# x blocks in the four-block output products, and group 0 on the same scheme: a fused attention and maxout kernel

## The chip, the cores and the metric

The kernel runs on one core of a Trainium2 chip. Its engines work side by side, each through its own instructions in order: TensorE (PE, matrix products), VectorE (DVE), ScalarE (ACT), GpSimd (POOL), and SyncE (SP), which here only issues transfers. PE's weight loads are listed apart as PEld. The metric is the device time of one execution in microseconds.

## The reference

Attention first, token by token, over 4 batches, 8 heads, 768 tokens and a head dimension of 48; then a feed-forward part over the 3072 tokens, with d_model 384 and d_ff 768:

```python
f = 1.0 / (1.0 + np.exp(-f_logit))
for t in range(S):
    state = f[:, :, t, :, None] * state + np.einsum('bhd,bhe->bhde', k[:, :, t], v[:, :, t])
    y[:, :, t] = np.einsum('bhd,bhde->bhe', q[:, :, t], state)
x = y.transpose(0, 2, 1, 3).reshape(B * S, H * D)
h = np.maximum(np.maximum(x @ w1, x @ w2), x @ w3)
out = h @ w_out
```

## The kernel before

**Units and groups.** Attention is cut into 24 units u of 128 rows (64 tokens of two batches). Four units make a group g of 512 tokens, and the feed-forward part works group by group, one group behind the attention: while the units 8 to 11 are worked, PE also does the feed-forward part of group 1, and so on. Group 0's part (`ffn_first`) is spread over the startup and the units 4 to 7; group 5's runs alone at the end.

**A unit** goes through `scan` (DVE, L329), `after` and `before` (the decays into keys and queries; POOL L340, L351, DVE L347), `pairs` (PE L392, DVE L395 applies the mask: tile at), `values` (PE L411), `sums` (PE L436, the state's increment), `finish` (PE L500) and `pack`. `sums` multiplies by ks, the keys by tokens, which DVE makes by 32x32 transposes in `keys_by_blocks` (L382): a unit has four blocks n of four transposes, the blocks 2 and 3 of unit u being made while unit u is worked, and L436's first two matmuls need blocks 0 and 1, the third needs block 3.

**The feed-forward weights.** The three input weights lie in w_in[0..2], six blocks of 128 columns each. w_in[1] and w_in[2] are stored less w_in[0], so that max(x w1, x w2, x w3) = x w1 + max(0, x w2', x w3'). The part x w1 is linear and goes straight to the output: `linear` multiplies w1 by w_out (PE L745) into w_nat, and w_lin is w_nat with its rows in the order of the packed x. So the output of a group is hm @ w_out + x @ w_lin, where hm holds the maxima, in six blocks of 128. Weights can arrive as pairs of 32-bit words; they are rounded on the chip by `round_begin` and `round_end` in 24 pieces, 18 of w_in and 6 of w_out: for pieces from number 3 on with two ACT operations (L240, L241) and one of DVE (L254), for the pieces below with two of DVE (L251, L252); then POOL adds (L258).

**Seven products for eight.** In groups 1 to 5 a product is taken two blocks by two blocks with Strassen's scheme in Winograd's form: seven block products, with sums of blocks made ahead. `inputs_by_pairs` does so for hm (PE L836; steps named start, plain, fifth, sixth, seventh, third, fourth for each of the three block pairs n). `fourth(n)` ends a pair: DVE takes the two maxima (L886, L887), and POOL makes four sums of the pair's blocks (`sums_of_hm`, L596, 128x256 each, into the places s1, s2, s4 in w_in[1] and into the blocks themselves). `outputs_by_pairs` (PE L609) then multiplies hm by w_out in seven products, with three hm pairs each, and adds x @ w_lin by four plain products of three x blocks each. The banks a, b and c of PSUM take the products in an order in which one bank's sum is used on: ACT reads bank a out (`read`, L614), while the next product is added on the same bank; DVE (`add`, L617) and POOL (L662) add the parts into the output. The weights' differences (w_mix) are made once by `mix` (POOL, L587).

**Group 0** uses plain products (`product`, PE L537; the maxima DVE L767), then `linear`, then `outputs` (PE L563), nine matmuls of 128x384 for each of four units, with `mix_in` and `mix` on POOL beside them.

**What sets the order.** It is written out by hand. The feed-forward part is a generator that yields the cost of each step; `fill(ns)` draws steps from it until a budget is used up, and stands between the steps of the units. The budgets are EARLY for units 4 to 7 and PART after. Every engine's queue keeps the order in which the program issues, so DVE works its maxima, its transposes and its scans strictly one after the other.

Of the kernel before, what the change touches and what calls it, by code (L numbers as in the profile page):

```python
# [46 lines left out]
C = 64  # L47
# [8 lines left out]
def kernel(  # L56
# [33 lines left out]
    def fast():  # L90
        ctx = ExitStack()
        with ctx:
# [137 lines left out]
            BY_VECTOR = 3  # L230
# [3 lines left out]
            def round_begin(n):  # L234
                if n in raw:
                    lo, hi = words(n)
                    top = tops[:, n % 4].bitcast(U32)
                    if n >= BY_VECTOR:

                        nc.scalar.activation(top.bitcast(FP32), hi.bitcast(FP32), AF.Sign)  # L240
                        nc.scalar.mul(top.bitcast(FP32), top.bitcast(FP32), -2.0)  # L241

                    rest = rests[:, n % 3].bitcast(U32)
                    nc.scalar.activation(rest, lo, AF.Copy, scale=2.0 ** -29)
                    halfway[n] = (top, rest)

            def round_end(n):
                if n in raw:
                    (top, rest), (_, hi) = halfway.pop(n), words(n)
                    if n < BY_VECTOR:  # L250
                        nc.vector.tensor_scalar(top, hi, 3, 0x3FFFFFF8, op0=ALU.logical_shift_left, op1=ALU.bitwise_and)  # L251
                        nc.vector.scalar_tensor_tensor(top, hi, 0xC0000000, top, op0=ALU.bitwise_and, op1=ALU.bitwise_or)  # L252
                    else:
                        nc.vector.scalar_tensor_tensor(top, hi, 3, top, op0=ALU.logical_shift_left, op1=ALU.bitwise_xor)  # L254

                    dst = pieces[n][0].bitcast(U32)
                    by = lambda t: t.rearrange("p (a c) -> p a c", a=dst.shape[1])
                    nc.gpsimd.tensor_tensor(dst, by(top), by(rest), op=ALU.add)  # L258
                    raw.pop(n)
# [250 lines left out]
            def by_halves(xT):  # L510

                return xT[:, 0:NK].rearrange("p k t -> p (k t)").rearrange("p (two k t) -> p two k t", two=2, k=NK)
# [14 lines left out]
            def bank(in_tr=False):  # L527
                if in_tr:
                    return ps_tr.tile([128, TOK], FP32, name="tr")
                return ps_f.tile([128, TOK], FP32, name="p")  # L530
# [26 lines left out]
            def outputs(hm, xT, i):  # L557
                p = bank()
                t = slice(i % 2 * UT, (i % 2 + 1) * UT)
                terms = [(hm[:, j, i * UT:(i + 1) * UT], w_out[:, j, :]) for j in range(NJ)]  # L560
                terms += [(by_halves(xT)[:, i // 2, k, t], w_nat[:, k, :]) for k in range(NK)]
                for n, (lhsT, rhs) in enumerate(terms):
                    nc.tensor.matmul(p[:, 0:DM], lhsT=lhsT, rhs=rhs, start=(n == 0), stop=(n == NJ + NK - 1))  # L563
                    if n % NK == NK - 1:
                        if n == NJ + NK - 1:
                            o = o_four[:, i]
                            nc.scalar.copy(o, p[:, 0:DM])
                            store(i, o)
                        yield NK * DM * COLUMN

            HJ, HD = NJ // 2, DM // 2
            corner = lambda k, n: w_out[:, k::2, n * HD:(n + 1) * HD]
            w_mix = [keep.tile([128, HJ, HD], FP32, name="mix")] + [w_in[2][:, :, n * HD:(n + 1) * HD] for n in range(4)]
            s_mix = [w_in[1][:, n, :].rearrange("q (jj t) -> q jj t", jj=HJ) for n in range(NK)]
            partial = [w_in[0][:, n, 0:DM] for n in range(NK)]
            pairs_of = lambda t: t.rearrange("q (p c) -> q p c", p=2)  # L580

            def mix(n):

                dst, x, y = ((w_mix[2], corner(1, 1), corner(0, 1)), (w_mix[0], corner(0, 1), corner(0, 0)),
                             (w_mix[1], corner(1, 1), w_mix[0]), (w_mix[3], corner(1, 0), w_mix[1]),
                             (w_mix[4], w_lin[:, :, 0:HD], w_lin[:, :, HD:]))[n]
                nc.gpsimd.tensor_tensor(dst, x, y, op=ALU.subtract)  # L587

            def sums_of_hm(hm, jj):

                first, second = ([hm[:, 2 * jj + k].rearrange("q (p n t) -> q n p t", p=2, n=2)[:, n] for n in range(2)]
                                 for k in range(2))
                s1, s2, s4 = (pairs_of(t[:, jj]) for t in s_mix)
                for dst, x, y, op in ((s1, first[1], second[1], ALU.add), (s2, s1, first[0], ALU.subtract),
                                      (first[1], first[0], first[1], ALU.subtract), (s4, second[0], s2, ALU.subtract)):
                    nc.gpsimd.tensor_tensor(dst, x, y, op=op)  # L596

            def outputs_by_pairs(g, hm, xT):
                tile_of = lambda p, n: slice((2 * p + n) * UT, (2 * p + n + 1) * UT)
                A = lambda k, n: lambda p: hm[:, k::2, tile_of(p, n)]  # L600
                X = lambda n: lambda p: xT[:, 0:NK, tile_of(p, n)]
                s1, s2, s4 = (lambda p, t=t: t[:, :, p * UT:(p + 1) * UT] for t in s_mix)
                lin = [w_lin[:, :, n * HD:(n + 1) * HD] for n in range(2)]
# [3 lines left out]
                def into(b, p, lhs, rhs):  # L607
                    for k in range(HJ):
                        nc.tensor.matmul(b[:, p * HD:(p + 1) * HD], lhsT=lhs(p)[:, k], rhs=rhs[:, k],  # L609
                                         start=id(b) not in begun, stop=(k == HJ - 1), skip_group_check=True)  # L610
                        begun.add(id(b))

                def read(b, n):
                    nc.scalar.copy(partial[n], b[:, 0:DM])  # L614
# [4 lines left out]
                COST = HJ * HD * COLUMN  # L619
                a, b, c = bank(), bank(True), bank(True)  # L620
                into(b, 0, X(0), lin[0])
                yield COST
                into(b, 1, X(0), lin[0])
                yield COST
                into(a, 0, A(0, 0), corner(0, 0))
                yield COST
                into(b, 0, A(1, 0), corner(1, 0))
                yield COST
                into(a, 1, A(0, 0), corner(0, 0))
                read(a, 0)  # L630
                yield COST
                into(b, 1, A(1, 0), corner(1, 0))
# [3 lines left out]
                yield COST  # L636
                into(a, 0, s2, w_mix[1])
                yield COST
                into(a, 1, s2, w_mix[1])
                read(a, 1)  # L640
                yield COST
                d = b if last else c
                into(c, 0, s1, w_mix[0])
# [4 lines left out]
                into(d, 1, s1, w_mix[0])  # L648
# [5 lines left out]
                into(a, 0, A(0, 1), w_mix[2])  # L654
                yield COST
                into(a, 1, A(0, 1), w_mix[2])
                yield COST
                into(a, 0, X(1), lin[1])
                yield COST
# [3 lines left out]
                if last:  # L663
                    store_part(g, 1, 1)
                yield COST
                into(c, 0, X(0), lin[1])
                yield COST
                into(d, 1, X(0), lin[1])
                yield COST
                into(a, 0, A(1, 1), w_mix[3])  # L670
                yield COST
                into(a, 1, A(1, 1), w_mix[3])
# [3 lines left out]
                into(a, 0, X(1), w_mix[4])  # L676
                yield COST
                into(a, 1, X(1), w_mix[4])
# [3 lines left out]
                yield COST  # L682
                into(c, 0, s4, corner(1, 1))
# [3 lines left out]
                into(d, 1, s4, corner(1, 1))  # L687
# [67 lines left out]
            def ffn_first(xT):  # L755
# [18 lines left out]
                for a in range(NK):  # L774
                    if a < 2:
                        for n in range(2 * NK + 2):
                            place(placed[a].bitcast(FP32), w_in[a + 1], n)
                    for cost in linear(a):
                        round_to(rounded[0] + 1)
                        yield cost  # L780
                for n in range(2 * NK + 2):
                    place(w_lin, w_nat, n)
                made = iter([lambda n=n: mix_in(n) for n in range(4)] + [lambda n=n: mix(n) for n in range(5)])
                for i in range(GRP):
                    for n, cost in enumerate(outputs(hm, xT, i)):
                        if i or n:
                            next(made, lambda: None)()
                        if i == GRP - 1 and n == 1 and 1 in packed:
                            sums_of_x(1)
                        yield cost  # L790
# [33 lines left out]
            def inputs_by_pairs(g, hm, xT):  # L824
# [57 lines left out]
                def fourth(n):  # L882
                    into(A[n], n, w_two[1][:, 1], t4)
                    yield COST
                    into(A[n], n, w_two[1][:, 2], t5)
                    nc.vector.scalar_tensor_tensor(out(n, 0), out(n, 0), 0.0, two(A[n]), op0=ALU.max, op1=ALU.max)  # L886
                    nc.vector.scalar_tensor_tensor(out(n, 1), out(n, 1), 0.0, u3, op0=ALU.max, op1=ALU.max)  # L887
                    sums_of_hm(hm, n)
                    yield COST
# [48 lines left out]
            EARLY = 2360  # L938
            PART = (33 * TOK + 22 * HJ * HD) * COLUMN / (5 * GRP)
# [408 lines left out]
```

## Time and profile before

| | |
|---|---|
| median of 3 runs | 423.31 us (423.26 to 423.86) |
| the profiled execution's own time | 423.43 us |
| its span, first to last instruction | 421.7 us |
| PE busy | 402.8 us, 96% |
| DVE, POOL, ACT busy | 264.5, 235.2, 180.2 us |
| group 0's outputs | 98.2 to 127.06 us |
| group 1, 2, 3 | to 187.47, 247.98, 308.49 us |
| group 4, group 5 | to 366.10, 416.60 us |

The stages are read from the timeline by PE's lines: a group goes from its first input product (L836) to the last output product (L609). The granted clock of PE is 0.996 over the span. A matmul of the program with 32-bit operands shows as two records in the trace. A row of the timeline gives start, duration, engine, line, operation, written and read tiles, and behind "x" how many records it gathers; in brackets stand the idle time of the engine ahead of it and what ended that.

### The profile page before, as it was taken

How to read it: one execution, taken by the hardware profiler on the slowest of the kernel's cores; microseconds unless marked ns; L12 is line 12 of the kernel's file. 1: busy time of each engine (PE TensorE's matmuls, PEld its weight loads, DVE VectorE, ACT ScalarE, POOL GpSimd, SP SyncE). 2: the span in 40 equal slices, each digit the busy share in tenths (PEclk: the TensorE clock that was granted, in tenths of full speed). 3: DMA queues.
4: the chain of work that ended last, by engine and by line, in shares of the span. 5: the costliest groups of instructions: out<-in, count | busy, mean ns of one | idle time of the engine just before them, and what ended most of it. 6: DMA issues, size and time to landing. Idle time of an engine off the chain costs nothing.

```text
span 421.7 us, 11556 instructions
## 1 busy us (share of the span) xinstructions
PE 402.8 (96%) x4650; PEld 338.5 (80%) x4650; DVE 264.5 (63%) x515; ACT 180.2 (43%) x414; POOL 235.2 (56%) x262
## 2 busy tenths in 40 slices
PE   4978899899999999999999999999999999999995
PEld 3756765466668888998889988889988889988994
DVE  6986594843597699868789867889764730002300
ACT  2478676632114442425531444442254524576210
POOL 2189554621988676376586357576556960435600
PEclk9999999999999999999999999999999999999998
DMA  8999897782547654277645276635473010542002
GB/s 169 232 266 284 236 258 112 121 170 67 102 85 129 87 116 66 60 106 101 117 104 95 56 113 87 144 79 89 64 144 91 11 54 9 158 140 75 2 19 60
DMA packets 175129, 47.20 MB, mean 112 GB/s; under 512 B 154016, under 2 KB 172768, under 8 KB 175072
## 3 DMA queue, kind: packets, MB, share of 16 engines
q1 hardware_dynamic: 171600, 45.61, 52.0%
q10 hardware_dynamic: 3472, 0.81, 0.9%
q8 instruction: 37, 0.61, 0.6%
q14 instruction: 20, 0.16, 0.1%
HBM read 37.75 MB, written 4.72 MB: 101 GB/s over the span
## 4 chain that ended last, share of the span: by engine, by line
PE 86%; SPq 5%; DVE 3%; POOL 2%; issue 1%; ACT 1%; DMA 1%; DVEq 0%; POOLq 0%
PE p L836 19%; PE tr L836 16%; PE p L609 15%; PE tr L609 12%; PE p L563 6%; PE p L537 5%; PE p L745 3%; PE y L500 3%; PE y L411 3%; SPq L164 2%; PE a L392 2%; SPq L174 2%; PE y L436 2%; POOL w_in L258 1%; DMA placed<-in_moe_w_dram 1%
## 5 line engine op out<-in xcount | busy, mean ns | idle before, releaser
L836 PE MATMUL tr<-xT,placed 128*128 128x256 f32 x300 | 73.3, 385 | 0.0
L382 DVE STREAM_TRANSPOSE ks<-kh 32x128 f32<-32x128 f32 x224 | 67.7, 302 | 4.6 <-POOL kh L340 1.0
L836 PEld LDWEIGHTS tr<-xT,placed 128*128 128x128 f32 x300 | 55.6, 190 | 9.1 <-ACT hm L844 1.4
L836 PE MATMUL p<-xT,placed 128*128 128x256 f32 x180 | 45.0, 381 | 0.0
L537 PE MATMUL p<-xT,w_in 128*128 128x256 f32 (+1 forms) x108 | 34.4, 459 | 4.9 <-DVE hm L767 2.2
L836 PEld LDWEIGHTS p<-xT,placed 128*128 128x128 f32 x180 | 33.8, 190 | 4.7
L329 DVE TENSOR_TENSOR_SCAN r<-gate,from_one 128x520 f32<-128x520 f32 x24 | 31.3, 1306 | 8.9 <-ACT gate L308 5.9
L617 DVE TENSOR_TENSOR o<-tr,w_in 128x384 f32<-128x384 f32 (+1 forms) x11 | 5.7, 515 | 48.8 <-PE tr L609 43.5
L340 POOL TENSOR_TENSOR kh<-kt,r 128x512 f32<-128x512 f32 x16 | 28.7, 1796 | 10.6 <-DVE kt L296 10.6
L596 POOL TENSOR_TENSOR w_in<-hm 128x256 f32<-128x256 f32 x15 | 10.9, 727 | 40.5 <-DVE hm L887 40.5
L854 POOL TENSOR_TENSOR hm<-hm,rest_bits 128x512 f32<-128x512 f32 x15 | 22.7, 1514 | 19.2 <-ACT hm L844 19.2
L506 ACT COPY xT<-y 64x256 f32<-64x256 f32 (+1 forms) x60 | 22.1, 369 | 24.1 <-PE y L500 23.4
L347 DVE TENSOR_TENSOR_SCAN prod<-gate,from_inv 128x520 f32<-128x520 f32 x24 | 31.9, 1329 | 0.0
L395 DVE TENSOR_TENSOR at<-a,mask 128x512 f32<-128x512 f32 x24 | 16.5, 688 | 24.2 <-PE a L392 23.9
L836 PE MATMUL p<-w_in,placed 128*128 128x256 f32 x120 | 30.0, 379 | 0.0
L537 PEld LDWEIGHTS p<-xT,w_in 128*128 128x128 f32 x108 | 19.3, 190 | 13.0 <-issue 6.2
L258 POOL TENSOR_TENSOR w_in<-top_bits,rest_bits 128x384 uint32<-128x384 uint32 x18 | 21.8, 1218 | 13.5 <-DVE top_bits L254 8.0
L879 DVE TENSOR_TENSOR hm<-tr,hm 128x512 f32<-128x512 f32 x15 | 10.2, 681 | 29.3 <-PE tr L836 19.3
L662 POOL TENSOR_TENSOR o<-top_bits,w_in 128x384 f32<-128x384 f32 x5 | 5.1, 1018 | 41.6 <-ACT w_in L614 41.6
L614 ACT COPY w_in<-p 128x384 f32<-128x384 f32 x15 | 7.2, 480 | 47.3 <-PE p L609 47.3
L280 ACT ACTIVATE raw<-top_bits 128x384 f32<-128x384 f32 x48 | 25.3, 526 | 0.4
L836 PEld LDWEIGHTS p<-w_in,placed 128*128 128x128 f32 x120 | 22.8, 190 | 3.1
(155 smaller groups left out, 888.4 us busy)
## 6 DMA issues: line engine op xcount, KB each, us to landing
raw<-in_moe_w_dram SPq DMA_DIRECT2D x24, 384.0 KB, 4.2
v_ld<-in_v_dram SPq DMA_DIRECT2D x48, 96.0 KB, 3.3
placed<-in_moe_w_dram SPq DMA_DIRECT2D x12, 384.0 KB, 5.7
out_dram<-o SPq DMA_DIRECT2D x46, 96.0 KB, 2.2
placed<-in_moe_w_out_dram SPq DMA_DIRECT2D x6, 384.0 KB, 5.9
raw<-in_moe_w_out_dram SPq DMA_DIRECT2D x6, 384.0 KB, 3.3
f_ld<-in_f_logit_dram SPq DMA_DIRECT2D x32, 64.0 KB, 2.6
k_ld<-in_k_dram SPq DMA_DIRECT2D x32, 64.0 KB, 2.5
```

The costliest lines, as they stand in the source:

```text
L258: nc.gpsimd.tensor_tensor(dst, by(top), by(rest), op=ALU.add)
L280: nc.scalar.activation(over, size, AF.Relu, scale=(-1 / HI_MIN, 1.0)[step - 1], bias=(1.0, -HI_END * (1 - 2.0 ** -24))[step - 1], accum_ou ...
L329: nc.vector.tensor_tensor_scan(r[:, 0:LEN][:, ::-1], flat(gate)[:, ::-1], flat(from_one)[:, ::-1], 1.0, op0=ALU.mult, op1=ALU.max)
L340: (nc.vector if u < BY_ROWS else nc.gpsimd).tensor_tensor(kh.rearrange("p h a t -> p a h t"), kt, by_batch(r[:, 1:LEN + 1].rearrange("p (x ...
L347: nc.vector.tensor_tensor_scan(flat(prod), flat(gate_tiles[u % 2]), flat(from_inv[u % 2]), 1.0, op0=ALU.mult, op1=ALU.max)
L382: nc.vector.transpose(ks[n * 32:(n + 1) * 32, :, par, e0:e0 + 32], kh[p0:p0 + 32, :, a, t0:t0 + 32])
L506: nc.scalar.copy(xT[o, :, t0 + a * C:t0 + (a + 1) * C], y[i, a, 0:HP * C].rearrange("p (h t) -> p h t", h=HP))
L537: nc.tensor.matmul(p if w < TOK else p.rearrange("p (two t) -> p two t", two=2), lhsT=w_in[i][:, kt, j * 128:(j + 1) * 128], rhs=x[:, t.st ...
L563: nc.tensor.matmul(p[:, 0:DM], lhsT=lhsT, rhs=rhs, start=(n == 0), stop=(n == NJ + NK - 1))
L609: nc.tensor.matmul(b[:, p * HD:(p + 1) * HD], lhsT=lhs(p)[:, k], rhs=rhs[:, k], start=id(b) not in begun, stop=(k == HJ - 1), skip_group_c ...
L836: nc.tensor.matmul(b[:, j * HALF:(j + 1) * HALF], lhsT=w[:, (2 * n + j) * 128:(2 * n + j + 1) * 128], rhs=x, start=begin and j == 0, stop= ...
L854: nc.gpsimd.tensor_tensor(out(n, 0), out(n, 0), first, op=ALU.add)
```

## The change

In the groups 1 to 5 the first two of the three x blocks become a fourth block pair in each of the seven output products: their sums are made like those of hm (`sums_of_pair`), on DVE, two in `fourth(1)` and two in `fourth(2)`; the differences of w_lin's blocks are made in group 1 by `mix_x`, on DVE. The third x block stays plain. In the two first hm products the blocks of the last hm pair stand behind those of all others ("early" and "rest"). The s1 product now stands before the s2 product.

Group 0 drops `outputs` and uses `outputs_by_pairs` with x plain, with its hm sums made during `linear` and its stores put out later, by `store_late` in group 1. `mix` goes from POOL to DVE, right behind `linear`, and `mix_in` goes into four steps of group 0's outputs. The w_out pieces are rounded by the two-operation way of DVE, two pieces a step. EARLY goes from 2360 to 2270, and PART follows the new number of products.

```diff
-            BY_VECTOR = 3
+            BY_VECTOR = (*range(3), *range(3 * NJ, 4 * NJ))
...
-                nc.gpsimd.tensor_tensor(dst, x, y, op=ALU.subtract)
+                nc.vector.tensor_tensor(dst, x, y, op=ALU.subtract)
+
+            def mix_x(n):
+
+                of = lambda k, c: w_lin[:, k, c * HD:(c + 1) * HD]
+                dst, x, y = ((x_mix[2], of(1, 1), of(0, 1)), (x_mix[0], of(0, 1), of(0, 0)),
+                             (x_mix[1], of(1, 1), x_mix[0]), (x_mix[3], of(1, 0), x_mix[1]),
+                             (w_mix[4][:, 2], of(2, 0), of(2, 1)))[n]
+                nc.vector.tensor_tensor(dst, x, y, op=ALU.subtract)
+
+            def sums_of_pair(x0, x1, *sums, part=slice(0, 4), engine=nc.gpsimd):
+
+                first, second = ([x.rearrange("q (p n t) -> q n p t", p=2, n=2)[:, n] for n in range(2)] for x in (x0, x1))
+                s1, s2, s4 = (pairs_of(t) for t in sums)
+                for dst, x, y, op in ((s1, first[1], second[1], ALU.add), (s2, s1, first[0], ALU.subtract),
+                                      (first[1], first[0], first[1], ALU.subtract), (s4, second[0], s2, ALU.subtract))[part]:
+                    engine.tensor_tensor(dst, x, y, op=op)
...
+                mixed = g > 0
+                order = [*range(HJ - 1), *[HJ] * mixed, HJ - 1]
+                A = lambda k, n: lambda p: [(xT[:, k] if jj == HJ else hm[:, 2 * jj + k])[:, tile_of(p, n)] for jj in order]
...
-                into(a, 0, A(0, 0), corner(0, 0))
-                yield COST
-                into(b, 0, A(1, 0), corner(1, 0))
-                yield COST
-                into(a, 1, A(0, 0), corner(0, 0))
+                early, rest = slice(len(order) - 1), slice(len(order) - 1, None)
+                for p in range(2):
+                    into(a, p, A(0, 0), C(0, 0), early)
+                    yield COST - PART_COST
+                    into(b, p, A(1, 0), C(1, 0), early)
+                    yield COST - PART_COST
+                for p in range(2):
+                    into(a, p, A(0, 0), C(0, 0), rest)
                 read(a, 0)
...
-                into(a, 0, s2, w_mix[1])
-                yield COST
-                into(a, 1, s2, w_mix[1])
-                read(a, 1)
-                yield COST
                 d = b if last else c
-                into(c, 0, s1, w_mix[0])
+                into(c, 0, s1, T(0))
...
+                into(a, 0, s2, T(1))
                 yield COST
-                into(a, 1, A(0, 1), w_mix[2])
+                into(a, 1, s2, T(1))
+                read(a, 1)
+                yield COST
+                into(a, 0, A(0, 1), T(2))
...
-                    for cost in linear(a):
-                        round_to(rounded[0] + 1)
+                    for n, cost in enumerate(linear(a)):
+                        round_to(rounded[0] + 2)
+                        if a and n < 2:
+                            jj = 2 * (a - 1) + n
+                            if jj < HJ:
+                                sums_of_hm(hm, jj)
                         yield cost
...
-                for i in range(GRP):
-                    for n, cost in enumerate(outputs(hm, xT, i)):
...
+                for n in range(5):
+                    mix(n)
+                for n, cost in enumerate(outputs_by_pairs(0, hm, xT)):
+                    if 3 <= n < 7:
+                        mix_in(n - 3)
+                    yield cost
...
                     sums_of_hm(hm, n)
+                    if n:
+                        sums_of_pair(xT[:, 0], xT[:, 1], *s_of_x(xT), part=slice(2 * n - 2, 2 * n), engine=nc.vector)
+                    if g == 1:
+                        for i in range(3 * n, min(3 * n + 3, 5)):
+                            mix_x(i)
                     yield COST
...
-            EARLY = 2360
-            PART = (33 * TOK + 22 * HJ * HD) * COLUMN / (5 * GRP)
+            EARLY = 2270
+            PART = (33 * TOK + 64 * HD) * COLUMN / (5 * GRP)
```

## The prediction

> **What bounds the kernel now.** First the page's busy shares, then the chain that ended last, then PE's waits, then the stretches of the program, and last the timeline around the place where the change puts its new work. The page says that PE is the bound, and that VectorE (DVE) is not, on average:
>
> ```profile
> PE 402.8 (96%) x4650; PEld 338.5 (80%) x4650; DVE 264.5 (63%) x515; ACT 180.2 (43%) x414; POOL 235.2 (56%) x262
> ...
> PE 86%; SPq 5%; DVE 3%; POOL 2%; issue 1%; ACT 1%; DMA 1%; DVEq 0%; POOLq 0%
> ```
>
> The answer on stretches, one line for the group 3 (group 2 reads the same), shows no idle time of PE at all, and DVE at 49.24 of 60.51 us:
>
> ```profile
> 247.98:308.49 60.51, 60.51 (x777) 53.99 (x777) 49.24 (x107) 23.93 (x56) 37.76 (x41) 1.00 0.55 96
> ```
>
> So a matmul less is time less, and a wait that PE does not have now is time more. The timeline where group 3's outputs begin (start, duration, engine, line) shows how close the nearest wait is:
>
> ```profile
> 280.10 0.69 DVE L879 TENSOR_TENSOR hm<-tr,hm 128x512 f32<-128x512 f32 x1 [0.70 <-PE tr L836]
> ...
> 280.80 1.26 DVE L382 STREAM_TRANSPOSE ks<-kh 32x128 f32<-32x128 f32 x4
> ...
> 282.81 2.11 PE L609 MATMUL tr<-w_in,xT 128*128 128x192 f32 x12
> ...
> 284.83 0.68 DVE L886 SCALAR_TENSOR_TENSOR hm<-hm,p 128x512 f32<-128x512 f32 x1
> 285.43 0.68 DVE L887 SCALAR_TENSOR_TENSOR hm<-hm,top_bits 128x512 f32<-128x512 f32 x1
> 285.56 0.30 PEld L609 LDWEIGHTS p<-w_out,hm 128*128 128x128 f32 x2 [0.28 <-DVE hm L886]
> ...
> 286.14 1.28 DVE L382 STREAM_TRANSPOSE ks<-kh 32x128 f32<-32x128 f32 x4
> 286.25 0.72 POOL L596 TENSOR_TENSOR w_in<-hm 128x256 f32<-128x256 f32 x1 [3.93 <-DVE hm L887]
> 287.06 0.74 POOL L596 TENSOR_TENSOR w_in<-w_in,hm 128x256 f32<-128x256 f32 x1
> ...
> 287.58 0.63 PE L436 MATMUL y<-v_ld,ks 64*64 64x48 f32 x32
> ...
> 288.09 1.48 DVE L347 TENSOR_TENSOR_SCAN prod<-gate,from_inv 128x520 f32<-128x520 f32 x1
> ...
> 288.43 1.67 POOL L596 TENSOR_TENSOR w_in<-hm,w_in 128x256 f32<-128x256 f32 x1
> ```
>
> Three things are to be seen. From 280.10 to 287.42 DVE has no gap: third maximum (L879), transposes, at, gate, scan, reciprocal, L886, L887, transposes. The last four transposes end at 287.42, and PE's L436, which multiplies by their result, starts at 287.58: a margin of 0.16 us. And the last POOL sum takes 1.67 instead of 0.73, ending 0.53 after DVE's scan: two engines, both reading two SBUF operands, took turns.
>
> **The change, part by part.** Durations are of the profiled execution, whose time is 423.43 us (span 421.7), 0.1 above the median 423.31. I forecast on 423.43 and count the 0.1 as nothing; 0.2%, or 0.85 us, is about what a measurement here can tell from no change.
>
> 1. *Fewer matmuls, groups 1 to 5.* A program matmul of 128x192 is two records; twelve records take 1.95 us in the chain ("171.29 1.95 PE tr L609 x12"), so 0.325 each. 64 instead of 66 in each of five groups: 10 x 0.325 = **-3.25**.
> 2. *Group 0.* 36 matmuls of 128x384 at 6.00 us for 18 records, nine matmuls ("101.77 6.00 PE p L563 x18"): 0.667 each, 24.0. Now 66 x 0.325 = 21.45: **-2.55**. Its hm sums (12 POOL sums of 0.73) go into the linear part from 87 us on; the five mixes, now on DVE at 0.5 to 0.7 (an estimate from L254's 0.55 for 128x384 and L617's 0.55), lie at 95.9 to 100.3, where DVE stands idle 6.88 before its L395 at 101.84. The eight late stores of group 0 on SP stand behind v loads that are wanted a unit later. All of this is hidden by PE's outputs; uncovered it would be some 3 us.
> 3. *A later read of the last hm pair.* L886's 0.28 wait in the timeline, in groups 1 to 3 (six matmul records take 1.39 instead of 1.14): 3 x 0.25 = **-0.75**. The last pair's matmuls now come behind L411 and L436.
> 4. *Startup.* EARLY moves the fills; PE's stall of 0.92 at 74.64 behind DVE's L767 should go. Against that, rounding of the six w_out pieces takes two DVE operations (L251 0.60, L252 0.56) for one (L254, 0.55 to 0.80). Between -1.2 and 0, and I take **-0.6**.
> 5. *Reads of bank a that lose their cover.* A read by ACT between two products on one bank costs 0.20 to start (402.73 to 402.93), 0.48 for L614, 0.06 back: 0.74. Since the s1 product now stands before s2, the read of s2 is followed at once by the next product on the bank. Group 0: 0.74, and 0.20 for the copy that its first matmul waits for: **+0.94**. Groups 1 to 3: L500 and L392 come between (1.07): nothing. Group 4: L500 alone (0.49): +0.25. Group 5: +0.74. Together **+0.99**. The next read has two matmuls (0.65) as cover instead of six: 0.1 in each of five groups, **+0.5**; in group 4 ACT has range checks (L278, L280, 0.5 each) queued ahead of it: between 0 and 1.5, taken as **+1.0**.
> 6. *New work on DVE: x sums and mix_x.* Two sums of 128x256 behind L887 of the second and of the third block pair, in every group; in group 1 also three and two subtractions of 128x192. Nearest rows: L767's 128x256 at 0.412, L617's 128x192 at 0.358, both with one operand in PSUM; I use 0.38 and 0.33. They stand ahead of the ks transposes on DVE, in order, and L436 waits for those.
>  Group 3: the first two delay L879 by 0.76 less its idle 0.70, 0.06. The next two add 0.76. L436 itself is due earlier by one matmul and the stall, 0.325 + 0.28, and had 0.16 of margin: 0.44 net. Stall 0.06 + 0.76 + 0.44 = **1.26**, in groups 2 and 3 each. Group 1 has the five subtractions as well: 0.3 at the L436 of u=10 (its transposes end at 150.52, L436 at 151.23) and 0.70 + 0.76 + 0.44 = 1.9 at the next, about 2.2. Sum without any collision **4.7**. Group 4's last unit and group 5 have no transposes there: nothing.
>  With collisions: POOL starts its four 0.73 sums on the same L887, at the same moment. The second x sum of the first pair depends on the first, so one POOL sum slips between: +0.73, of which nothing is covered any more (idle 0.70 used up); the second pair takes 0 to 0.73. Groups 2 and 3: 0.79 + 0.76 + 0.36 + 0.44 = **2.35** each (2.0 to 2.7). Group 1: three subtractions with two POOL sums between, 0.3 to 1.65 at u=10; then four operations with three POOL sums between them, 0.76 + 0.66 + 3 x 0.73 - 0.72 = 2.9, and 2.9 + 0.76 + 0.36 + 0.44 = 4.5 at the next: **5.2** (4.4 to 6.5). Sum **9.9**. What else stands behind the sums on DVE has room: L395's at would end at 283.6, and PE's L411 wants it at 286.4; s1 of the last hm pair on POOL would come by about 288.2, wanted after L436.
>
> The evidence for collisions is the row of 1.67 above, and others in startup:
>
> ```profile
> 75.11 1.19 POOL L258 TENSOR_TENSOR w_out<-top_bits,rest_bits 128x384 uint32<-128x384 uint32 x1 [6.09 <-DVE top_bits L254]
> ...
> 75.35 1.36 DVE L254 SCALAR_TENSOR_TENSOR top_bits<-placed,top_bits 128x384 uint32<-128x384 uint32 x1
> ```
>
> L254 took 0.55 at 74.41 and 1.36 here, ending 0.41 after POOL's add: DVE waits for POOL, too. So I take the sum with collisions, at a little less than its full size, since operations that follow without a dependence may keep their turn.
>
> The Trainium skill ("SBUF — State Buffer", section "Who interferes with whom") says that a DVE instruction with two SBUF inputs contends with a GpSimd instruction that reads SBUF, and that the loser is blocked for the winner's whole instruction. L767 and L617 with their one SBUF input are then the wrong rows to price these sums by: by the rule the stalls come near the upper sum and the time near 429.6, by those two rows the time is 424.4.
>
> **Sum.** Without part 6: -3.25 - 2.55 - 0.75 - 0.6 + 0.94 + 0.99 + 0.5 + 1.0 = -3.7. With 9.9: +6.2, with 4.7: +1.0. I forecast 428.5, that is +5.1, stalls of 8.8.
>
> **The rivals.**
> - *No collision.* POOL's sums would have to start after the x sums, which is against the 0.11 us between L887's end and L596's start. 423.43 + 1.0 = 424.4.
> - *The transposes are in time* (the other side). At L436 of units 11, 15 and 19 nothing is waited for, and the saved matmuls are what counts: 423.43 - 3.7 = 419.7. For it: DVE is 63% busy, and the trace has gaps of 0.70 and 0.45 before L879 and L886. Against it: the chain from L879 to the transposes has none. It decides for "faster" once the stalls of groups 1 to 3 add up to less than 3.7 - 0.85 = 2.85 us.
> - *DVE late in startup.* The extra 6 x 0.4 of rounding falls before L767's maxima, on which PE's L537 waits (it already loses 2.2 in all): 428.5 + 2.4 + 0.6 = 431.5.
>
> **How the numbers follow.** Collisions, 426 to 431: 0.58. No collision, 423.5 to 425.3: 0.15, a third of it within 0.2%. Transposes in time, 419.5 to 422: 0.20. Startup: 0.07. The range 421.5 to 431 leaves out most of the third and the fourth case; the likeliest case alone is 426 to 431. Faster 0.20, same 0.06, slower 0.74.
>
> **What the profile after would show.** Right: PE's L436 of u=11, 15, 19 waiting for ks L382, 2 to 5 us each; DVE's new sums at over 1 us in part, POOL's at 1.1; group 0's outputs some 24 us long instead of 28.9; groups 2 and 3 longer than 60.51; ACT's read of bank a followed by an idle PE in groups 0 and 5. Wrong: x sums at 0.4 with L436 at once behind L411 (second rival), or a stall of some 1.2 (first).

## The result and the profile after

The changed kernel takes 439.47 us (median; 438.83 to 440.71) against 423.59 (423.26 to 424.14) for the kernel before on the same chip: the ratio is 1.0382, 95% interval 1.0365 to 1.0398. The forecast was slower, 428.5 with a range up to 431, so the direction was right and the size far off. The spans of the two profiles, 437.9 and 421.7 us, differ by 16.2; what follows accounts for these.

The page of the kernel after, busy shares, the granted clock in the 40 slices (9 is 90% of full speed or more), and the chain that ended last. Its line numbers differ: L618 is now what L609 was (output products), L852 is L836, L902 and L903 are L886 and L887 (the two maxima), L623 is L614 (`read`), L586 holds all sums of pairs (on POOL for hm, on DVE for x), and L578 is `mix_x`.

```profile
PE 408.3 (93%) x4690; PEld 350.9 (80%) x4690; DVE 290.0 (66%) x553; ACT 174.9 (40%) x403; POOL 241.2 (55%) x270
...
PEclk9999999999999988999998999998999999999998
...
PE 78%; SPq 6%; DVE 4%; ACT 3%; DMA 3%; issue 2%; POOL 1%; ACTq 0%; DVEq 0%
```

PE is busy 5.5 us longer, although it has 2 program matmuls less in each of five groups, and it holds 78% of the chain instead of 86%; the row of the clock has slices of 8. The waits of PE (waiting line, releaser, us in total, times, longest) show the wait that was forecast:

```profile
PE y L436 <- DVE ks L382: 9.1, 8, 2.6
...
PE p L618 <- ACT w_in L623: 1.1, 2, 0.6
PE p L759 <- DVE hm L781: 0.9, 1, 0.9
...
PE p L618 <- ACT rest_bits L623: 0.6, 1, 0.6
```

But 9.1 us of idle time and more busy time in spite of less work do not fit a forecast that had everything in the waits. The timeline of group 2, where its output products begin (they do at 229.72), shows the place:

```profile
233.05 0.68 DVE L902 SCALAR_TENSOR_TENSOR hm<-hm,p 128x512 f32<-128x512 f32 x1
...
233.38 0.69 PE L411 MATMUL y<-at,v_ld 64*64 64x64 f32 x32
233.65 0.68 DVE L903 SCALAR_TENSOR_TENSOR hm<-hm,top_bits 128x512 f32<-128x512 f32 x1
...
233.90 0.27 PE L436 MATMUL y<-v_ld,ks 64*64 64x48 f32 x4
234.25 0.42 DVE L586 TENSOR_TENSOR xT<-xT 128x256 f32<-128x256 f32 x1
234.47 0.77 POOL L586 TENSOR_TENSOR w_in<-hm 128x256 f32<-128x256 f32 x1 [4.24 <-DVE hm L903]
234.58 0.94 DVE L586 TENSOR_TENSOR s_last<-xT 128x256 f32<-128x256 f32 x1
...
235.54 1.28 DVE L382 STREAM_TRANSPOSE ks<-kh 32x128 f32<-32x128 f32 x4
...
236.22 0.31 PE L436 MATMUL y<-v_ld,ks 64*64 64x48 f32 x2 [2.05 <-DVE ks L382]
...
236.87 0.66 PE L436 MATMUL y<-v_ld,ks 64*64 64x48 f32 x26 [0.34 <-DVE ks L382]
...
237.47 1.62 PE L618 MATMUL tr<-w_out,hm 128*128 128x192 f32 x4
...
238.88 0.85 PE L618 MATMUL tr<-w_in,xT 128*128 128x192 f32 x2
```

The x sums (DVE L586) stand between the maxima and the transposes, and L436 waits for the transposes, as forecast. New are the last two lines: four records of a 128x192 product take 1.41 us until the next product begins, where the same form takes 0.75 behind an attention step in a run below. The answer on stretches around it (length, busy times of PE, PEld, DVE, ACT, POOL, then the granted clock, DMA share, GB/s) says why:

```profile
233.70:236.20 2.50, 0.47 (x32) 0.34 (x21) 2.44 (x7) 0.00 (x0) 1.65 (x3) 1.00 0.50 63
236.20:238.20 2.00, 1.64 (x30) 1.46 (x31) 1.95 (x4) 0.00 (x0) 1.98 (x4) 0.83 0.58 104
238.20:240.20 2.00, 2.00 (x8) 2.00 (x8) 1.99 (x5) 0.00 (x0) 2.00 (x2) 0.50 0.63 200
240.20:242.20 2.00, 2.00 (x12) 2.00 (x11) 1.17 (x4) 0.48 (x1) 1.42 (x2) 0.82 0.00 0
```

After the wait PE works at half its clock for a while, 3.41 us each time when the stretches are cut to 0.2 us. From the mean clock of the stretches (0.96 over group 1's inputs, 38.49 us; 0.94 over the outputs of groups 1 to 3, 30.02, 29.47 and 29.48 us), this costs some 6.9 us, about 1.7 (half of 3.41) for each of four falls.

So the 16.2 us divide as follows. The time from L411 to the next feed-forward product is 1.08 in the kernel before, everywhere. After, it is 3.00 and 4.73 in group 1, 4.09 and 1.32 in group 2, 4.08 and 1.32 in group 3: 12.06 us more in all. The low clock adds 6.9. What is left, -2.8, is the gain of everything else.

### The profile page after: what moved, and what is told of

It is laid out like the page before. It is cut to its first block, busy times and chain, and to the rows that moved or that the text cites. A ratio compares the mean times of both kernels' runs of the same rounds, so it can differ in the third digit from the quotient of the medians.

```text
span 437.9 us, 11671 instructions
## 1 busy us (share of the span) xinstructions
PE 408.3 (93%) x4690; PEld 350.9 (80%) x4690; DVE 290.0 (66%) x553; ACT 174.9 (40%) x403; POOL 241.2 (55%) x270
## 4 chain that ended last, share of the span: by engine, by line
PE 78%; SPq 6%; DVE 4%; ACT 3%; DMA 3%; issue 2%; POOL 1%; ACTq 0%; DVEq 0%
PE p L852 16%; PE tr L852 15%; PE p L618 15%; PE tr L618 12%; PE p L537 6%; PE p L759 3%; PE y L500 3%; PE y L411 2%; PE y L436 2%; SPq L164 2%; SPq L183 2%; SPq L174 2%; DMA f_ld<-in_f_logit_dram 2%; PE a L392 2%; PE tr L291 1%
## 5 line engine op out<-in xcount | busy, mean ns | idle before, releaser
L852 PE MATMUL tr<-xT,placed 128*128 128x256 f32 x300 | 74.9, 391 | 0.0
L852 PEld LDWEIGHTS tr<-xT,placed 128*128 128x128 f32 x300 | 56.5, 193 | 9.4 <-ACT hm L860 1.4
L852 PE MATMUL p<-xT,placed 128*128 128x256 f32 x180 | 45.2, 382 | 0.0
L340 POOL TENSOR_TENSOR kh<-kt,r 128x512 f32<-128x512 f32 x16 | 32.1, 2007 | 20.2 <-DVE kt L296 20.1
L329 DVE TENSOR_TENSOR_SCAN r<-gate,from_one 128x520 f32<-128x520 f32 x24 | 32.9, 1370 | 8.6 <-ACT gate L308 5.6
L537 PE MATMUL p<-xT,w_in 128*128 128x256 f32 (+1 forms) x108 | 34.3, 458 | 4.0 <-POOL w_in L729 2.2
L852 PEld LDWEIGHTS p<-xT,placed 128*128 128x128 f32 x180 | 34.0, 192 | 4.6
L339 POOL COPY ends<-r 128x8 f32<-128x8 f32 x24 | 6.7, 278 | 55.2 <-DVE r L329 55.2
L586 POOL TENSOR_TENSOR w_in<-hm 128x256 f32<-128x256 f32 x18 | 14.1, 782 | 40.1 <-DVE hm L903 40.1
L618 PE MATMUL p<-w_in,hm 128*128 128x192 f32 x144 | 31.1, 338 | 1.8 <-ACT w_in L623 1.1
L623 ACT COPY w_in<-p 128x384 f32<-128x384 f32 x15 | 7.2, 478 | 58.8 <-PE p L618 58.8
L347 DVE TENSOR_TENSOR_SCAN prod<-gate,from_inv 128x520 f32<-128x520 f32 x24 | 30.1, 1254 | 0.0
L852 PE MATMUL p<-w_in,placed 128*128 128x256 f32 x120 | 30.0, 379 | 0.0
L537 PEld LDWEIGHTS p<-xT,w_in 128*128 128x128 f32 x108 | 19.3, 190 | 11.8 <-issue 5.3
L618 PE MATMUL tr<-w_out,w_in 128*128 128x192 f32 x144 | 28.6, 326 | 0.0
L618 PE MATMUL p<-w_in,xT 128*128 128x192 f32 x124 | 27.0, 326 | 0.0
```

The lines of the kernel that those rows point to most:

```text
L329: nc.vector.tensor_tensor_scan(r[:, 0:LEN][:, ::-1], flat(gate)[:, ::-1], flat(from_one)[:, ::-1], 1.0, op0=ALU.mult, op1=ALU.max)
L340: (nc.vector if u < BY_ROWS else nc.gpsimd).tensor_tensor(kh.rearrange("p h a t -> p a h t"), kt, by_batch(r[:, 1:LEN + 1].rearrange("p (x ...
L347: nc.vector.tensor_tensor_scan(flat(prod), flat(gate_tiles[u % 2]), flat(from_inv[u % 2]), 1.0, op0=ALU.mult, op1=ALU.max)
L537: nc.tensor.matmul(p if w < TOK else p.rearrange("p (two t) -> p two t", two=2), lhsT=w_in[i][:, kt, j * 128:(j + 1) * 128], rhs=x[:, t.st ...
L586: engine.tensor_tensor(dst, x, y, op=op)
L618: nc.tensor.matmul(b[:, p * HD:(p + 1) * HD], lhsT=x, rhs=w, start=id(b) not in begun, stop=True, skip_group_check=True)
```

## The experiments

**Leaving the new DVE work out.** In the changed kernel, where two memsets fill tiles that nothing else writes now:

```diff
+            nc.gpsimd.memset(s_last, 0.0)
+            nc.gpsimd.memset(x_mix[3], 0.0)
...
                     sums_of_hm(hm, n)
-                    if n:
-                        sums_of_pair(xT[:, 0], xT[:, 1], *s_of_x(xT), part=slice(2 * n - 2, 2 * n), engine=nc.vector)
-                    if g == 1:
-                        for i in range(3 * n, min(3 * n + 3, 5)):
-                            mix_x(i)
```

> The sums of the x blocks and mix_x are left out (the x pair's products then read stale data); every matmul stays. Theory A: PE's waits at L436 (9.06 us in all in the profile after: 1.30 + 2.98 + 2.39 + 2.39) come from these operations, and each wait is followed by some 4 us at about half the granted clock, about 2 us each, 8 in all. Then both go: 439.5 - 9.1 - 8 = about 422.4, no wait at L436 over 0.2, granted clock back at 0.996. Rival B: the waits cost only themselves and the low clock has another cause (the new matmul order): 430.4, clock still 0.98. My forecast's sum without the waits was 419.7.

Measured: 422.58 us, 0.9974 of the kernel before (0.9962 to 0.9986); the clock 0.997. So the loss of 16.9 us comes from these 25 operations, which keep DVE busy for 18.0 us in the kernel after (L586 14.3, L578 3.7). Theory A holds, B falls. But the gain that then stands is 0.9 us, not 3.7. A part of the difference is still at L436: the time from L411 is 1.32 and 1.58 in each of groups 1 to 3, 2.2 us in all, without any x sum. L411 stands 3.67 us after the start of group 1's outputs instead of 4.25: the shorter budget between the attention steps (PART) and the one matmul less before L411 have brought L436 up against the transposes by themselves.

**Keeping PE busy in the wait.** The changed kernel with useless matmuls ahead of L436:

```diff
+            IDLE = {10: 3, 11: 7, 15: 5, 19: 5}
...
+                if u in IDLE:
+                    p = ps_a.tile([128, 2, 512], FP32, name="a")
+                    for _ in range(IDLE[u]):
+                        nc.tensor.matmul(p[:, 0, 0:256], lhsT=ident, rhs=from_one.rearrange("p x t -> p (x t)")[:, 0:256],
+                                         start=True, stop=True)
                 if u >= GRP:
                     sums(u)
```

> Nothing is taken away: PE gets 3, 7, 5 and 5 useless matmuls of 128x256 (about 0.43 us each) between L411 and L436 of units 10, 11, 15 and 19, where it stands idle now; their result goes into a bank that nobody reads. Theory A: the clock falls because PE idles; with PE busy in the same time the granted clock stays at 1.00 after L436 and the kernel gets faster by about 8 us, to 431 to 432, by doing more. Rival B (the low clock or slow matmuls come from something else at that place, transfers or the order of the matmuls): 439.5 or up to 2 more.

Measured: 433.92 us (433.08 to 435.21), 5.5 less than the changed kernel, with more work (8 less were expected). The timeline of PE in group 2 and the stretches behind it:

```profile
230.95 0.69 PE L413 MATMUL y<-at,v_ld 64*64 64x64 f32 x32
231.58 2.43 PE L420 MATMUL a<-from_one,ident 128*128 128x256 f32 x10
233.93 0.33 PE L443 MATMUL y<-v_ld,ks 64*64 64x48 f32 x6
234.46 0.66 PE L443 MATMUL y<-v_ld,ks 64*64 64x48 f32 x26 [0.21 <-DVE ks L382]
235.06 0.92 PE L625 MATMUL tr<-w_out,hm 128*128 128x192 f32 x4
235.81 0.49 PE L625 MATMUL tr<-w_in,xT 128*128 128x192 f32 x2
```

```profile
234.00:236.00 2.00, 1.79 (x39) 1.62 (x39) 1.95 (x4) 0.00 (x0) 1.98 (x4) 1.00 0.66 126
236.00:240.00 4.00, 4.00 (x26) 4.00 (x26) 3.90 (x11) 0.48 (x1) 3.22 (x3) 1.00 0.26 87
```

L420 is the filling; L443 stands for L436 and L625 for L618. The block from L411 on is as long as before the filling (4.11 against 4.09), but the next product runs at 0.75 for four records, and the clock is 1.00. Over the whole kernel the blocks came out 0.94 longer and the span 5.8 shorter, so the clock cost 6.7, near the 6.9 read from the stretches. The order of the other matmuls, the transfers and DVE's work are as they were; the low clock comes from PE's idle time.

**The same wait in the kernel before.** There the four transposes were made three times, and in another run two times, in units 11, 15 and 19:

```diff
-                    keys_by_blocks(u, 3)
+                    for _ in range(3 if u in (11, 15, 19) else 1):
+                        keys_by_blocks(u, 3)
```

> The kernel before, all else unchanged, with the four transposes of ks block 3 made three times over in units 11, 15 and 19: DVE brings ks 2.55 later, so PE should stand idle at L436 about 2.4 in each of groups 1 to 3, 3.0 of delay with the restart, 9 in all. Theory A (the idle time itself lowers the granted clock): 1.7 more for each, 423.5 + 9 + 5 = 437.5, clock about 0.985. Rival (the clock fell only in the changed kernel's order of matmuls): 432.5, clock 0.996.

> The same with the transposes made twice: ks 1.27 later, an idle time of about 1.1 in each of three groups, 1.7 of delay with the restart, 5 in all: 428.5 if the clock stays, as it did in two runs with waits of 1.0 to 1.4; 433.5 if it falls, as it did in the changed kernel after 0.96 + 0.34 at 150 us. Theory A leaves this open; the run tells what a short wait costs in this kernel.

Measured: 436.06 us (ratio 1.0288, 1.0269 to 1.0308), clock 0.985, with three waits of 1.68 + 0.36; and 427.70 us (1.0097, 1.0079 to 1.0116), clock 0.999, with three of 0.34 + 0.36. Stretches of the first of them, group 2, the wait being at 232.3 to 234.0:

```profile
232.00:234.00 2.00, 0.32 (x21) 0.19 (x10) 1.81 (x7) 0.00 (x0) 1.73 (x4) 1.00 0.68 87
234.00:236.00 2.00, 1.64 (x29) 1.42 (x30) 1.94 (x4) 0.00 (x0) 0.58 (x1) 0.71 0.69 147
236.00:238.00 2.00, 2.00 (x8) 2.00 (x8) 1.51 (x3) 0.14 (x1) 2.00 (x2) 0.50 0.38 129
238.00:240.00 2.00, 2.00 (x13) 2.00 (x12) 0.82 (x3) 0.34 (x1) 1.36 (x2) 0.94 0.00 0
```

The old order of matmuls does the same: half clock behind the wait. In the first run the blocks at L436 (from L411 to the next product) are 8.9 us longer in all, as expected, and the groups 1 to 3 together 12.8 (64.67, 64.78 and 64.78 against 60.41, 60.51 and 60.51). That leaves 3.9 for the clock; another 1.1 or so, half of the time that the clock is already low inside the blocks, is contained in the 8.9: 5.0 for three falls. (The span is 13.5 longer; 0.7 of it lies ahead of group 1.) In the second run the blocks are 1.31 longer each, 3.9 in all (5 expected), and each of the three groups is longer by just that: a short wait costs the delay at L436 and no clock.

**Is it a collision with POOL?** First try: DVE transposes with one operand in place of the x sums.

```diff
-                        sums_of_pair(xT[:, 0], xT[:, 1], *s_of_x(xT), part=slice(2 * n - 2, 2 * n), engine=nc.vector)
+                        s1x, s2x, s4x = s_of_x(xT)
+                        for dst, x in (((s1x, xT[:, 0, 0:HALF]), (s2x, xT[:, 1, 0:HALF])), ((xT[:, 0, 0:HALF], xT[:, 1, 0:HALF]),
+                                       (s4x, xT[:, 1, 0:HALF])))[n - 1]:
+                            nc.vector.transpose(dst, x)
```

> The four x sums of each group are replaced by DVE transposes of the same 128x256 size with one operand in SBUF (the values are not the sums); mix_x and POOL's sums stay. Theory A with collisions: the transposes take about 0.37 each, POOL's sums beside them 0.73, the waits of groups 2 and 3 fall from 2.39 to about 1.3 (0.44 + 0.76 + 0.06) each, group 1's from 4.3 to about 2.5; whether the clock still drops after 1.3 us of waiting decides between 434 and 436 (drops stay) and 427 (no drop). Rival, no collision: the DVE operations are just slow, waits and time stay (439.5).

Measured: 436.70 us (436.18 to 441.10), which decides nothing: the third transpose wrote xT's first tiles, which the early hm products read, so PE waited for it there ("PE p L618 <- DVE xT L909: 9.1, 5, 3.2"). An experiment that replaces an operation must write just what the operation writes. The second try does:

```diff
+                        second = [xT[:, k].rearrange("q (p n t) -> q n p t", p=2, n=2)[:, 1] for k in range(2)]
...
+                                       ((second[0], second[1]), (s4x, xT[:, 1, 0:HALF])))[n - 1]:
```

> As the earlier run with one-operand transposes of 128x256 in place of the x sums, but the one that stands for the in-place sum writes only the second tile of each half, as the sum does, so that the early product does not wait for it. Theory with collisions: the DVE pair takes 0.8 instead of 1.9 and 1.4, POOL's sums 0.73, the delay at L436 of groups 2 and 3 falls from 3.0 to about 1.5 each; time 427 to 434, by whether the clock still falls behind the shorter waits. Rival, no collision: 439.5.

Measured: 428.42 us (427.39 to 428.92), clock 0.998 in the profile and 0.993 in two of the four executions. Group 2 again, now without two-operand sums on DVE:

```profile
219.67 0.76 DVE L910 STREAM_TRANSPOSE xT<-xT 128x256 f32<-128x256 f32 x2
...
227.62 0.44 DVE L910 STREAM_TRANSPOSE xT<-xT 128x256 f32<-128x256 f32 x1
...
227.85 0.73 POOL L586 TENSOR_TENSOR w_in<-hm 128x256 f32<-128x256 f32 x1 [3.32 <-DVE hm L903]
...
227.99 0.40 DVE L910 STREAM_TRANSPOSE s_last<-xT 128x256 f32<-128x256 f32 x1
```

The same place of the kernel after, first pair of sums:

```profile
224.62 1.27 POOL L357 TENSOR_TENSOR state<-st,ends 128x384 f32<-128x384 f32 x1
225.13 1.91 DVE L586 TENSOR_TENSOR xT<-xT 128x256 f32<-128x256 f32 x2
225.86 0.90 POOL L586 TENSOR_TENSOR w_in<-hm 128x256 f32<-128x256 f32 x1
```

The two pairs of transposes take 0.76 and 0.84 where the sums take 1.91 and 1.36. The block at L436 is 2.40 instead of 4.09: collisions are 1.7 of its 3.0 us of delay, and without them the clock does not fall behind the waits of groups 2 and 3 (0.37 + 0.34), nor, in this execution, behind the 1.42 + 0.34 of group 1. The transposes' price of 0.4 is also what the first sum of the second pair took, which began 0.22 ahead of POOL's (0.42 at 234.25); the next one, beside POOL, took 0.94. So a sum is not slow by itself, and the rival "no collision" is out.

**The transposes ahead of the maxima.** In the changed kernel, nothing left out:

```diff
+                    if u >= 2 * GRP:
+                        keys_by_blocks(u, 3)
                     fill(part)
-                    keys_by_blocks(u, 3)
+                    if u < 2 * GRP:
+                        keys_by_blocks(u, 3)
```

> The four transposes of block 3 of ks are put on DVE ahead of the last maxima (before the fill instead of behind it) from unit 8 on; the x sums stay where they are, behind the maxima. Theory A: L436 no longer waits (the transposes end about 2 us ahead of it), the last pair's maxima come 1.3 later but their product stands behind L436; waits and clock drops go: 421 to 423, as without the sums, a little slower than the kernel before or faster than it by up to 2. Rival C: DVE is simply too full there, and the wait moves to the last pair's product or to L411: 428 to 432.

Measured: 426.54 us, 1.0072 (1.0050 to 1.0094), clock 0.999, between the two forecasts. The wait did not move to the last pair's product or to L411, which rival C says: L436 itself still waits, 3.6 us in all. Groups 2 and 3 are back to 25.4 us of outputs, with blocks of 1.71 and 1.31. But group 1's blocks are 2.99 and 3.32: the mix_x operations stand further ahead on DVE and delay everything behind them, and the scan (1.24 to 1.43) still stands ahead of the transposes.

**One part of the change alone.** Group 0 as changed, the order of the products as changed, but x plain in groups 1 to 5:

```diff
-                mixed = g > 0
+                mixed = False
...
-                    if n:
-                        sums_of_pair(xT[:, 0], xT[:, 1], *s_of_x(xT), part=slice(2 * n - 2, 2 * n), engine=nc.vector)
-                    if g == 1:
-                        for i in range(3 * n, min(3 * n + 3, 5)):
-                            mix_x(i)
+                    if g == 1 and n == 0:
+                        nc.vector.tensor_tensor(w_mix[4], w_lin[:, :, 0:HD], w_lin[:, :, HD:], op=ALU.subtract)
...
-            PART = (33 * TOK + 64 * HD) * COLUMN / (5 * GRP)
+            PART = (33 * TOK + 66 * HD) * COLUMN / (5 * GRP)
```

> Only one part of the change: group 0 on the paired scheme, mix on DVE, the last hm pair late, s1 before s2, rounding and EARLY as changed; but in groups 1 to 5 the x blocks stay plain (66 matmuls, no x sums, one subtraction of 128x576 in group 1 in place of the five). By my forecast's terms without the x sums and with 10 matmuls more: 423.5 - 3.7 + 3.25 = 423.1; by the run without x sums (422.6) plus 3.25 less the waits that the smaller PART makes (about 2): 423.8. If group 0's part brings its full 2.55: 421 to 422.

Measured: 427.28 us, 1.0095 (1.0071 to 1.0118), against 423.1 to 423.8 expected. The expectation missed what the new order of products does by itself. The outputs of groups 1 to 3 take 26.9 us instead of 25.5: the block at L436 is 1.89 (0.81 more), because the early products are cheaper and let the attention steps come sooner (L411 3.34 us after the start of group 1's outputs, 4.25 in the kernel before), and the read of bank a, 0.57, is not covered in any of these groups, since the steps fall elsewhere. Group 0's end lies at 125.76 (kernel before 126.90), so startup and group 0 together gain 1.1 us in these two executions.

**Three moves.** Transposes ahead of the scan; mix_x where DVE waits for PE at the end of group 0; s2 before s1 in groups 0, 4 and 5, where the sums are long done:

```diff
+                    keys_by_blocks(u, 3)
                     if n < NU:
                         if n < BY_ROWS:
                             sigmoids(n)
                         scan(n)
...
                     fill(part)
-                    keys_by_blocks(u, 3)
...
-                    if g == 1:
-                        for i in range(3 * n, min(3 * n + 3, 5)):
-                            mix_x(i)
...
                 into(c, 0, s4, C(1, 1))
+                if not mixed:
+                    for i in range(5):
+                        mix_x(i)
...
+                if g in (0, 4, 5):
+                    yield from s2_first()
                 into(c, 0, s1, T(0))
...
+                if g not in (0, 4, 5):
+                    yield from s2_first()
```

> Three moves in the changed kernel, nothing left out: ks block 3 goes on DVE ahead of the gate transpose and the scan; the five mix_x go to the end of group 0's outputs, where DVE waits for PE; in groups 0, 4 and 5 the s2 product stands before s1 again, so that the read of bank a is covered. By theory A (waits at L436 from what stands ahead of ks, and the clock falling behind them) no wait at L436 is left, also not the 0.24 and 0.5 that were left without any x sums; granted clock 0.997 or more; 422.6 (the run without x sums) - 2.2 - 1.7 = 418.7, between 418 and 421, faster than both kernels. Rival C (DVE is too full, the wait moves to L411 or to the last pair's product): 423 or more.

Measured: 419.58 us, 0.9896 of the kernel before (0.9882 to 0.9911), so faster than both kernels; the clock is 1.00. Group 2's timeline:

```profile
221.44 0.69 DVE L395 TENSOR_TENSOR at<-a,mask 128x512 f32<-128x512 f32 x1
222.16 1.28 DVE L382 STREAM_TRANSPOSE ks<-kh 32x128 f32<-32x128 f32 x4
...
224.50 0.69 PE L411 MATMUL y<-at,v_ld 64*64 64x64 f32 x32
...
225.01 0.63 PE L436 MATMUL y<-v_ld,ks 64*64 64x48 f32 x32
...
226.81 0.42 DVE L586 TENSOR_TENSOR xT<-xT 128x256 f32<-128x256 f32 x1
...
227.04 0.78 POOL L586 TENSOR_TENSOR w_in<-hm 128x256 f32<-128x256 f32 x1 [5.68 <-DVE hm L913]
...
227.14 0.95 DVE L586 TENSOR_TENSOR s_last<-xT 128x256 f32<-128x256 f32 x1
```

The transposes end 1.6 us ahead of L436, and PE has no wait at L436 left. The x sums collide with POOL's work as they did (0.42 and 0.95 here, 1.91 for the first pair), and it costs nothing, because PE waits for nothing that stands behind them. The outputs of groups 1 to 3 take 24.87 us where the kernel before takes 25.52.

## Why the prediction was right and wrong

By the forecast's own parts:

| part | forecast | measured |
|---|---|---|
| 1 and 3, fewer matmuls, late read of the last pair, less 0.1 for the read of bank a | -0.80 in each of groups 1 to 3 | -0.65 (24.87 against 25.52, in the run without waits) |
| 2 and 5, group 0 | -2.55 + 0.94 = -1.61 | -0.69 (28.04 us against 28.73, to the start of group 1) |
| 4, startup | -0.6 | -0.25 (group 0's outputs begin at 97.92 instead of 98.17); on average -0.8 (97.86 over the eight profiles with the new startup, 97.02 to 98.82; 98.64 over three with the old) |
| 1 and 5, output stages of groups 4 and 5 | -0.65 + 0.25 + 0.1 + 1.0 = +0.7 and -0.65 + 0.74 + 0.1 = +0.2 | +0.2 and +0.4 |
| 6, delay at L436 | 8.8 | 12.06 |
| not in the forecast: clock | 0 | 6.9 |

*The mechanism of part 6 was right*, its place, its releaser and its doubling by collisions with POOL too. It was undersized by 3.3 us (the forecast took 8.8 of its own upper sum of 9.9). Its DVE terms had 0.76 + 0.73 for the first pair of sums and 0.76 + 0.36 for the second; measured 1.91 and 1.36, as the first sum, too, can wait for a POOL operation: at 225.13 it took 1.05 and outlasted POOL's L357, which ended at 225.89. The matmuls of L436 come back in two steps, 0.65 us apart (at 236.22 and 236.87), which no term had. And the blocks of the units 14 and 18 are 0.24 longer as well, as they are without the x sums. (The 0.11 us that the prediction reads between L887 and POOL's first sum is 0.14 in its own rows; nothing rests on the difference.)

*The step that failed* is the sum's premise, "a wait that PE does not have now is time more", taken as the wait's length. A wait of PE here has a second price, 1.7 us of clock for each of four waits, 6.9 in all. With the 3.3 by which the delay at L436 was undersized and the 0.9 by which the gain was oversized, this makes up the 11 us between 428.5 and 439.47. The profile before could not show it: PE has no such wait behind its startup. The Trainium skill has a page on it, "TensorE: Matmul & The Clock Gate" (section "What's actually happening"): PE's clock is at half after an idle window of about 3.4 us, the window being free-running. The prediction did not weigh it. The traces agree with the length and with the free run: the low clock lasts 3.41 us, and the falls keep a grid of 3.413 us (last section). But the window need not be idle: 1.68 + 0.36 us of waiting, with small matmuls around it, was enough in three cases of three in the kernel before, and PE was busy for 1.37 of the 3.41 us ahead of each fall.

*The gain was oversized by 0.9 us*, 2.8 for 3.7, by these two profiles. In part 2 the term of 0.667 for a 128x384 matmul came from the chain's row of 18 records in 6.00 us, which includes the slower first product behind an attention step. The timeline has six records, three matmuls, from 103.74 to 105.67: 0.643 each, 23.2 instead of 24.0 in all. So the move to 66 small matmuls is worth 1.7. Of this the uncovered read takes 0.6 ("PE p L618 <- ACT rest_bits L623: 0.6, 1, 0.6"), near the forecast's 0.74, and the first product some 0.2 (97.92 to 99.09 for three matmuls), as forecast. The range checks, taken at 1.0 in group 4, came out as a wait of 0.56 ("375.79 0.92 PE L618"). In part 4 the stall of 0.92 at L537 did not go; it stands at `linear` now ("PE p L759 <- DVE hm L781: 0.9, 1, 0.9").

*The rivals.* "No collision" is refuted by the durations. "The transposes are in time" was false for the changed kernel, but its number, 419.7, is nearly what the kernel with the three moves reaches (419.58). That it fits so closely is partly chance, since that kernel also covers the read in group 0 again (27.14 us instead of 28.04). The saved matmuls are real, once nobody waits behind the new sums: 24.87 against 25.52 in each of groups 1 to 3. "DVE late in startup" did not happen; L537's waits fell from 2.2 to 1.3.

## What to carry to other kernels

Before work is put on an engine that is idle on average, look up what stands behind it in that engine's queue, who waits for that, and with how much margin; here that margin was 0.16 us. Moving the waited-for transposes ahead of the new work cut a loss of 3.8% to 0.7%; putting them further ahead, with `mix_x` and the s2 products moved too, made it a gain of 1.0%. Waits of 2 us and more on PE cost the delay itself here and about 1.7 us each in clock on top. A step that shortens PE's work also shortens what hides other engines, so the margins of the waits nearby have to be taken anew.

## What the runs showed of the hardware

- Waits of 1.68 + 0.36 us or longer at L436 brought the granted clock to 0.50 in each of the six cases (three in the kernel after, of 2.05 to 2.64 + 0.34; three in the kernel before with slower transposes), from 0.8 to 1.5 us behind the restart and for 3.41 us. Waits of 0.34 + 0.36 did so in none of three.
- The falls keep a grid of their own. In the kernel after the clock falls at 152.19, 172.67, 237.52 and 302.38, and once more behind PE's end at 435.50: 6, 19, 19 and 39 steps of 3.413 us. In the kernel before with the transposes made three times it falls at 169.98, 234.83 and 299.68: 19 and 19 steps, while the restarts of PE lie 64.77 and 64.78 apart, not 64.85. So a fall comes at points of a grid that does not follow the program. That it hangs on how little PE did in the 3.41 us ahead of such a point, and not on the length of one wait, fits all falls here.
- This settles most of what lies in between. The kernel after waited 0.96 + 0.34 at 150.66, and its clock fell; the kernel with the transposes ahead of the maxima had the same two waits at 150.42 and 151.08, and its clock stayed at 1.00. The grid of the second, counted back from the fall behind its end (424.03), spreads the two waits over two stretches, where the kernel after has both in one. The stretches on their grids, first the kernel after, then the other:

```profile
148.78:152.19 3.41, 2.11 (x66) 1.67 (x66) 3.25 (x8) 0.82 (x3) 0.23 (x2) 1.00 0.69 182
152.19:155.60 3.41, 3.41 (x9) 2.71 (x9) 3.38 (x7) 0.12 (x1) 3.41 (x3) 0.50 0.71 184
```

```profile
147.55:150.96 3.41, 2.23 (x44) 1.57 (x42) 3.25 (x8) 1.19 (x4) 0.19 (x1) 1.00 0.69 145
150.96:154.37 3.41, 3.29 (x39) 2.93 (x40) 3.38 (x6) 0.58 (x1) 2.46 (x2) 1.00 0.87 244
```

- The limit itself stays open. Stretches of the grid with PE busy for 1.44 us or less were, from group 1 on and up to PE's end, always followed by half clock (nine of nine in all runs). Near 2.1 us both happened: 2.11 in the kernel after fell, 2.10 in the run with the second try of transposes (147.25 to 150.66) did not. Busy time alone is not the measure; what the small matmuls count for is not shown.
- Two DVE sums of 128x256 with both operands in SBUF took 1.91 beside POOL's work, two one-operand operations of the same size 0.76, and POOL's first sum beside them 0.90 in the one case and 0.72 in the other: both engines lose.
